# Order of the AV matmuls over two column tiles in a sliding-window attention and SwiGLU kernel

## The chip, the cores and the metric

The kernel runs on one core of a Trainium2 chip. The metric is the device time of one execution in microseconds (us). Times are medians over several executions. A profile is one execution taken by the hardware profiler; its span is about 1.7 us shorter than the timed figure of the same run. All runs quoted here were classed as fast (undisturbed) runs.

In the profile, PE is the TensorE's matmul stream and PEld its stream of weight loads; DVE is VectorE, ACT is ScalarE, POOL is GpSimd, and SPq is the queue from which SyncE issues DMAs. "L354" is line 354 of the kernel. The ends of matmuls are modelled, so everything below is argued from their starts.

## The reference

```python
def _attn_ref(q, k, v):                      # (8, 8, 576, 64), float32
    scores = (q @ k.transpose(0, 1, 3, 2)) / sqrt(64)
    mask = |pos_i - pos_j| <= 32             # a window of 65 positions
    attn = softmax(where(mask, scores, -1e9))
    return attn @ v

x = attention output, heads side by side     # (4608, 512)
out = (silu(x @ w_gate) * (x @ w_val)) @ w_out    # d_ff = 1536
```

## The kernel before

Queries are cut into blocks of 64, and each block needs 128 keys. Two query blocks make a *pair* `m`, with 36 pairs in all. The scores are computed transposed (keys on the partitions), passed through exp and multiplied with a 0/1 mask. The result `p` is then the stationary operand of the AV matmul: 128 keys x 64 queries. The moving operand is `v16`, 64 columns of V and two columns of ones, which give the softmax's denominator: 66 columns. The output of the pair's first query block (`i = 0`) goes to PSUM partitions 0-63, and that of the second (`i = 1`) to 64-127. The profile lists both kinds as 128*64 (128 rows x 64 columns of the array). The two kinds are called the two *column tiles* below.

```python
def pair_av(m, pool=None):
    p = pts.pop(m)
    o = (pool or ps_c).tile([128, 2, 512], FP32, ...)      # two halves of 512
    for i in range(2):
        b, t = divmod(2 * m + i, NT)
        for h in range(H):                                 # H = 8
            nc.tensor.matmul(
                out=o[64 * i:64 * i + 64, h // 4, 66 * (h % 4):66 * (h % 4) + 66],
                lhsT=p[:, place(b, h)[0], i, place(b, h)[1], :],
                rhs=v16[b % 2][:, t, h, :],
                start=True, stop=True)
    # VectorE: reciprocal of the denominators, then normalised x16[m]
    ...

def pair_xt(m, on_pe=False):     # x16[m] is turned into xT, by a DMA transpose or (early) on PE
    ...
```

The two halves of `o`, 512 floats a partition each and chosen by `h // 4`, are called banks below.

The scores (`s_ps`, L306) alternate between two *row* tiles (listed as 64*128: 64 rows x 128 columns), one matmul to each in turn. The rest of PE's work is the FFN: `gv_ps` (L391) and `ob` (L405), on the full 128 x 128 array with 512 columns. The FFN of a chunk of 512 tokens is interleaved with the attention of the next batch, in eight slots:

```python
for j in range(1, NCH):
    ffn1(j)                                       # 96 matmuls, gv_ps
    ...
    groups = {1: ((), (0, 1)), 3: ((0,), (2, 3)), 5: ((1, 2), (4,)), 7: ((3, 4), ())}
    for slot in range(8):
        at_a, at_s = groups.get(slot, ((), ()))   # AV of these pairs, scores of those
        done = [todo[i] for i in at_a if i < n]
        for i, m in enumerate(done):
            pair_av(m, ps_a if i else None)
        for i in at_s: ...pair_scores(todo[i])
        for m in done:
            pair_xt(m)
        ffn2_sub(j, slot // 2, slot % 2)          # 6 matmuls, ob
```

So AV matmuls come in blocks: 16 where one pair stands alone, 32 where two follow one another.

Of the kernel before, what the change touches and what calls it, by code (L numbers as in the profile page):

```python
# [132 lines left out]
def kernel(  # L133
# [12 lines left out]
    B, H, S, D = q.shape  # L146
# [4 lines left out]
    NT = S // 64  # L151
# [145 lines left out]
    def place(b, h):  # L297

        return (h % 4 // 2, 2 * (h // 4) + h % 2) if b < 2 else (h % 2, h // 2)
# [47 lines left out]
    def pair_av(m, pool=None):  # L347
        p = pts.pop(m)
        o = (pool or ps_c).tile([128, 2, 512], FP32, tag="a" if pool is ps_a else "c",
                                name="o_ps")  # L350
        for i in range(2):
            b, t = divmod(2 * m + i, NT)
            for h in range(H):
                nc.tensor.matmul(  # L354
                    out=o[64 * i:64 * i + 64, h // 4, 66 * (h % 4):66 * (h % 4) + 66],
                    lhsT=p[:, place(b, h)[0], i, place(b, h)[1], :],
                    rhs=v16[b % 2][:, t, h, :],
                    start=True, stop=True)
        ov = o[:, :, 0:264].rearrange("p a (h e) -> p a h e", e=66)
        r = rall[:, m, :].rearrange("p (a h) -> p a h", a=2)  # L360
        nc.vector.reciprocal(out=r, in_=ov[:, :, :, 64])  # L361
        x16s[m] = xpool.tile([128, 2, 4, D], FP16, tag="x", name="x16")
        nc.vector.tensor_tensor(out=x16s[m], in0=ov[:, :, :, 0:D],
                                in1=r.unsqueeze(3).to_broadcast([128, 2, 4, D]),
                                op=ALU.mult)
# [140 lines left out]
    quad_mask((2, 3), 1)  # L506
    idle_mms(4)
    pair_av(0)
    pair_av(1, ps_a)
    idle_mms(4)  # L510
    pair_av(2, ps_a)
    pair_av(3)

# [125 lines left out]
```

## Time and profile before

The median before is 341.45 us (341.18 to 341.92, 4 runs). The page of its profile (engines: busy time, share of the span and instructions; then the chain of work that ended last, as shares of the span by engine and by line):

```profile
span 339.8 us, 6448 instructions
PE 327.0 (96%) x2592; PEld 159.8 (47%) x2592; DVE 157.9 (46%) x288; ACT 155.9 (46%) x223; POOL 106.6 (31%) x139
...
PE 94%; DVE 1%; ACT 1%; DMA 1%; issue 1%; POOL 0%; POOLq 0%
PE gv_ps L391 55%; PE ob L405 27%; PE o_ps L354 4%; PE s_ps L306 3%; PE warm L437 2%; PE qk_ps L281 1%; ACT xT L262 1%; DMA xT<-x_1758 1%; PE ob L424 1%; DVE p_t L344 1%; DVE v_103 L265 0%; PE xt_ps L378 0%; DVE mask L202 0%; ACT osb L413 0%; DVE osb_4022 L265 0%
```

PE is the bound: it is on the chain for 94% of the span. The AV matmuls (`o_ps`, L354) are 4% of it, so no ordering of them can gain more than that.

The one DMA in the list of PE's waits (total us, times, longest), just before an FFN:

```profile
PE gv_ps L391 <- DMA xT<-x_1758: 0.3, 1, 0.3
```

The most telling view is the timeline of PE in one 16-block whose two query blocks fall in different batches, so that the two tiles read differently named V buffers (v_103 for `i = 0`, v_104 for `i = 1`). The columns are start, time from the first start to the last end, engine, line, operation and tiles, shapes and count; consecutive starts of the same kind are merged:

```profile
120.99 0.38 PE L405 MATMUL ob<-wo_128,hT 128*128 128x512 f16 x1
121.30 0.34 PE L354 MATMUL o_ps<-v_103,p_t 128*64 128x66 f16 x5
121.45 0.22 PE L354 MATMUL o_ps<-v_104,p_t 128*64 128x66 f16 x1
121.48 0.20 PE L354 MATMUL o_ps<-v_103,p_t 128*64 128x66 f16 x1
121.51 0.20 PE L354 MATMUL o_ps<-v_104,p_t 128*64 128x66 f16 x1
121.51 0.19 PE L354 MATMUL o_ps<-v_103,p_t 128*64 128x66 f16 x1
121.54 0.19 PE L354 MATMUL o_ps<-v_104,p_t 128*64 128x66 f16 x1
121.54 0.19 PE L354 MATMUL o_ps<-v_103,p_t 128*64 128x66 f16 x1
121.58 0.32 PE L354 MATMUL o_ps<-v_104,p_t 128*64 128x66 f16 x5
121.83 0.26 PE L306 MATMUL s_ps<-qT_102,kT_100 64*128 64x64 f16 x5
```

The program has eight v_103, then eight v_104. The chip started the first v_104 when five v_103 had started and three had not, and from there on it ran both tiles side by side. Matmuls of *different* column tiles overtook one another; within a tile the names do not tell the eight apart, and their order there is taken as the program's. The single starts of this block, in ns from its first:

```
i = 0:    0   52   88  120  152  181  215  248
i = 1:                          158  210  246  279  311  340  375  407
```

Counted from its own first start, each row has the same rhythm within 2 ns: 0, 52, 88, 120 or 121, 152 or 153, 181 or 182, 215 to 217, 248 or 249. A tile takes about 249 ns from the first to the last start of its eight matmuls, whether the other runs beside it or not. The second tile only starts 158 ns late, and 158 + 249 = 407. Around the block, the first AV matmul starts 309 or 310 ns after the `ob` before it, where one full-array matmul mostly starts 215 or 216 ns after another, and the next matmul starts 125 to 127 ns after the last AV start (all blocks of this profile from 50 us on, without the one at 60 us).

### The profile page before, as it was taken

The numbers are of one execution on the slowest core, as the hardware profiler recorded it, in microseconds if no ns is written. First come the engines' busy times: TensorE is split into PE (matmuls) and PEld (weight loads), VectorE is DVE, ScalarE is ACT, GpSimd is POOL, SyncE is SP. The second block draws the span as 40 slices with busy tenths as digits, with TensorE's granted clock in tenths as the row PEclk, the third lists the DMA queues.
The fourth block names the chain that finished last, engine by engine and source line by source line (L and its number), as shares of the span: only waits on it lengthen the run. The fifth ranks groups of instructions, "written<-read, shape, count | busy, mean of one in ns | idle before, by whom it ended". The sixth has DMA issues, their size and how long they took to land.

```text
span 339.8 us, 6448 instructions
## 1 busy us (share of the span) xinstructions
PE 327.0 (96%) x2592; PEld 159.8 (47%) x2592; DVE 157.9 (46%) x288; ACT 155.9 (46%) x223; POOL 106.6 (31%) x139
## 2 busy tenths in 40 slices
PE   6889999999999999999999999999999999999993
PEld 3444545444544454445444454455445544444442
DVE  3744365336624763466345644564446634403310
ACT  2964576535543464337333743373336443223321
POOL 8973875146204710463045503560000000000000
PEclk9999999999999999999999999999999999999997
DMA  7999999799969996999599949998530420020012
GB/s 274 169 212 301 212 158 200 126 131 111 147 148 149 99 136 138 131 129 129 151 125 127 130 122 130 152 108 150 111 62 33 106 65 1 33 93 0 2 63 70
DMA packets 152981, 41.92 MB, mean 123 GB/s; under 512 B 140528, under 2 KB 146416, under 8 KB 152944
## 3 DMA queue, kind: packets, MB, share of 16 engines
q0 software_dynamic: 100640, 16.52, 67.7%
q1 hardware_dynamic: 52304, 24.92, 31.4%
q8 instruction: 22, 0.36, 0.5%
q14 instruction: 15, 0.12, 0.1%
HBM read 37.75 MB, written 9.44 MB: 139 GB/s over the span
## 4 chain that ended last, share of the span: by engine, by line
PE 94%; DVE 1%; ACT 1%; DMA 1%; issue 1%; POOL 0%; POOLq 0%
PE gv_ps L391 55%; PE ob L405 27%; PE o_ps L354 4%; PE s_ps L306 3%; PE warm L437 2%; PE qk_ps L281 1%; ACT xT L262 1%; DMA xT<-x_1758 1%; PE ob L424 1%; DVE p_t L344 1%; DVE v_103 L265 0%; PE xt_ps L378 0%; DVE mask L202 0%; ACT osb L413 0%; DVE osb_4022 L265 0%
## 5 line engine op out<-in xcount | busy, mean ns | idle before, releaser
L398 DVE TENSOR_TENSOR hT<-ssb,gv_ps 128x512 f16<-128x512 f16 x108 | 74.3, 688 | 122.4 <-ACT ssb L397 122.1
L397 ACT ACTIVATE ssb<-gv_ps 128x512 f16<-128x512 f32 x108 | 64.5, 597 | 112.7 <-PE gv_ps L391 110.4
L391 PE MATMUL gv_ps<-xT,wg_126 128*128 128x512 f16 x432 | 110.8, 379 | 1.2 <-ACT xT L262 0.8
L391 PE MATMUL gv_ps<-xT,wv_127 128*128 128x512 f16 x432 | 110.9, 379 | 0.0
L405 PE MATMUL ob<-wo_128,hT 128*128 128x512 f16 x420 | 97.3, 380 | 0.0
L391 PEld LDWEIGHTS <-wv_127 128*128 128x128 f16 x432 | 42.3, 98 | 51.0
L391 PEld LDWEIGHTS <-wg_126 128*128 128x128 f16 x432 | 41.9, 98 | 51.6 <-issue 2.8
L405 PEld LDWEIGHTS <-hT 128*128 128x128 f16 x420 | 38.6, 98 | 43.6
L223 POOL DMA_DIRECT2D tok<-in_q_dram x30 | 25.4, 847 | 83.3 <-DMA qT_101<-tok 45.9
L312 ACT ACTIVATE p_t<-s_ps 128x1024 f16<-128x1024 f32 (+1 forms) x40 | 35.3, 937 | 12.3 <-PE s_ps L306 12.2
L413 ACT ACTIVATE osb<-ob 128x512 f32<-128x512 f32 x35 | 21.0, 600 | 41.7 <-PE ob L405 40.6
L223 POOL DMA_DIRECT2D tok<-in_k_dram x30 | 25.3, 843 | 21.3 <-DMA kT_99<-tok 5.0
L322 DVE TENSOR_TENSOR p_t<-p_t,mask 128x1024 f16<-128x1024 f16 x32 | 22.1, 692 | 13.8 <-ACT p_t L312 13.8
L354 PEld LDWEIGHTS <-p_t 128*64 128x64 f16 x576 | 15.4, 110 | 10.6 <-issue 5.9
L361 DVE RECIPROCAL rall<-o_ps 128x8 f32<-128x8 f32 x36 | 7.3, 204 | 21.1 <-PE o_ps L354 21.0
L437 PE MATMUL warm<-mask 128*128 128x512 f16 x26 | 8.9, 467 | 2.9 <-DVE mask L202 2.9
L242 POOL DMA_DIRECT2D v_103<-in_v_dram x12 | 11.4, 956 | 0.5 <-issue 0.5
L354 PE MATMUL o_ps<-v_103,p_t 128*64 128x66 f16 x288 | 10.1, 197 | 1.1 <-DVE p_t L344 1.1
L242 POOL DMA_DIRECT2D v_104<-in_v_dram x12 | 10.6, 896 | 0.0
L397 ACT ACT_TABLE_LOAD x8 | 10.3, 1283 | 0.1
L265 DVE COPY v_103<-v_103 64x512 f16<-64x512 f16 x26 | 9.9, 381 | 0.8
L265 DVE COPY v_104<-v_104 64x512 f16<-64x512 f16 x28 | 9.4, 335 | 0.9
(137 smaller groups left out, 156.3 us busy)
## 6 DMA issues: line engine op xcount, KB each, us to landing
out_dram<-osb SPq DMA_DIRECT2D x35, 256.0 KB, 2.4
tok<-in_q_dram POOLq DMA_DIRECT2D x24, 128.0 KB, 4.9
tok<-in_k_dram POOLq DMA_DIRECT2D x24, 128.0 KB, 5.0
qk_st<-in_q_dram SPq DMA_DIRECT2D x4, 576.0 KB, 6.9
qk_st<-in_k_dram SPq DMA_DIRECT2D x4, 576.0 KB, 8.7
v_103<-in_v_dram POOLq DMA_DIRECT2D x12, 128.0 KB, 5.4
wo_128<-in_moe_w_out_dram POOLq DMA_DIRECT2D x4, 384.0 KB, 21.3
v_104<-in_v_dram POOLq DMA_DIRECT2D x12, 128.0 KB, 4.2
```

The source lines that it names most:

```text
L223: nc.gpsimd.dma_start(out=t[0:n].rearrange("p (h d) -> p h d", d=D), in_=src[b].rearrange("h s d -> s h d")[128 * m:128 * m + n])
L242: nc.gpsimd.dma_start(out=dst[:, 2 * m, :, 0:D], in_=src[128 * m - 32:128 * m + 96])
L265: nc.vector.tensor_copy(out=o, in_=i)
L312: nc.scalar.activation(out=o, in_=s, func=AF.Exp, bias=0.0, scale=1.0 / float(D) ** 0.5)
L322: nc.vector.tensor_tensor(out=flat, in0=flat, in1=mask, op=ALU.mult)
L354: nc.tensor.matmul(out=o[64 * i:64 * i + 64, h // 4, 66 * (h % 4):66 * (h % 4) + 66], lhsT=p[:, place(b, h)[0], i, place(b, h)[1], :], rhs ...
L391: nc.tensor.matmul(out=gv[:, i, :], lhsT=w[:, g, 128 * fk:128 * fk + 128], rhs=xts[j][:, g, :], start=(g == 0), stop=(g == GS - 1))
L397: nc.scalar.activation(out=ssb, in_=gv[:, 0, :], func=AF.Silu, bias=0.0, scale=1.0)
L398: nc.vector.tensor_tensor(out=hts[j][:, fk, :], in0=ssb, in1=gv[:, 1, :], op=ALU.mult)
L405: nc.tensor.matmul(out=ob, lhsT=hts[j][:, fk, 128 * sub:128 * sub + 128], rhs=wo16[:, fk, :], start=(fk == 0), stop=(fk == FKS - 1))
L413: nc.scalar.activation(out=osb, in_=ob, func=AF.Copy, bias=0.0, scale=1.0)
L437: nc.tensor.matmul(out=ob, lhsT=mf[:, 0:128], rhs=mf[:, 0:512], start=True, stop=True)
```

## The change

The intent is to keep both column tiles busy all the time by giving each its next matmul in turn, instead of eight heads of one tile and then eight of the other.

```diff
-        for i in range(2):
-            b, t = divmod(2 * m + i, NT)
-            for h in range(H):
+        for h in range(H):
+            for i in range(2):
+                b, t = divmod(2 * m + i, NT)
                 nc.tensor.matmul(
                     out=o[64 * i:64 * i + 64, h // 4, 66 * (h % 4):66 * (h % 4) + 66],
```

No instruction is added or removed; only PE's order within L354 changes. Below, this order is called *strict turns*.

## The prediction

> **What bounds the kernel.** TensorE. The page gives PE 327.0 us of 339.8 (96%), and the chain that ended last is 94% PE; PE's waits sum to under 8 us, of which 0.3 after 120 us. The AV matmuls (o_ps, L354) are 4.4% of that chain. What shortens PE's AV stretches shortens the program nearly one for one, except where something else starts the next PE stretch.
>
> **AV now.** The 576 AV matmuls stand in 13 blocks of 32 (two pairs) and 10 of 16. By single starts in the timeline, a lone column tile steps every 32 ns: weight load, matmul 26 ns later, next weight load 2 ns later. But where the program changes tile, the second tile starts while the first still has three matmuls to run. The block at 121.30 us, whose two tiles read different v buffers, shows it: five v_103, then v_104 and v_103 in turns, two matmuls per 31 ns step, then five v_104 alone. So a 16-block is 5+3+5 = 13 steps (407 ns, first to last start), a 32-block 5+3+2+3+2+3+5 = 23 steps (726 ns). Part of the overlap is there already.
>
> **The change.** The order comparison shows the same instructions, with PE's order within L354 alone changed. In strict turns every step should carry two matmuls: 8 and 16 steps. The score matmuls (L306), which alternate row tiles, show the shape: starts 3 ns apart, then 26. With each block's start-up (steps of 52 and 36 ns, then 32), a 16-block takes 251 ns to its last start (saves 156), a 32-block 507 (saves 219). The 309 ns before the first AV start and 126 after the last stay. [...]
>
> **On the critical path.**
> - 11 blocks of 32 and 9 of 16 from 50 to 270 us, PE-bound: 11 x 0.219 + 9 x 0.156 = 3.8 us.
> - Blocks at 14.8 and 17.9 us: nothing. VectorE works without pause from the last masks (to 16.8) to x_413 (20.3), which gates the FFN at 21.48.
> - Block at 60.5 us: nothing. The FFN after it waits for ScalarE's xT.
> - At 131.6 us PE waited 0.33 us for the DMA of x_1758. PE comes earlier there, the DMA only in part: 0.3 us given back.
>
> 3.8 - 0.3 = 3.5 us: 341.3 - 3.5 = **337.8 us** (1.0% less), 80% range 336.6 to 339.3. Chances: faster by over 2% 0.01, within 2% 0.98, slower 0.01. Over 2% needs 6.8 us, more than alternation can remove.
>
> **What would show it.** L354 starts in couples 2 to 5 ns apart, every 30 to 32 ns; block time (first AV start to next PE instruction) from 852 to about 633 ns, and 535 to about 380. FFN and score stretches unchanged; first FFN still at about 21.5 us. The wait for xT's DMA from 0.33 to about 0.6 us.
>
> **What would make it wrong.** The couples now write one PSUM bank at once, where today's overlapping ones write different banks. [...] If they took turns, the gain would be zero or negative, as the present overlap would go too. Likewise if the look-ahead fails in strict turns. A small shift can also put other DMA transposes on the path (at 95.9 us xT's landing leads its use by about 0.2 us).

That the two tiles of a couple may write one bank at once was the assumption until experiment 3. The step of a lone tile is stated from single starts: over the block at 121.30 us its matmul starts 26 to 33 ns after its weight load (2 ns for the first), and the next load 1 to 3 ns after that.

## The result

The changed kernel takes 338.06 us (337.96 to 338.52, 4 runs) against 341.45 us. The ratio is 0.9902, 95% interval 0.9885 to 0.9919. Ratios here are the mean time of one kernel's fast runs over that of the other's of the same rounds, so they are not quite the ratios of the medians quoted. The prediction said 337.8 us.

The page after:

```profile
span 336.4 us, 6448 instructions
PE 322.8 (96%) x2592; PEld 155.0 (46%) x2592; DVE 158.1 (47%) x288; ACT 156.0 (46%) x223; POOL 106.2 (32%) x139
...
PE 90%; DMA 4%; DVE 2%; ACT 1%; issue 1%; SPq 1%
PE gv_ps L391 56%; PE ob L405 26%; PE o_ps L354 3%; PE s_ps L306 3%; DMA qk_st<-in_k_dram 2%; DMA xT<-x 2%; ACT xT L262 1%; PE qk_ps L281 1%; DVE p_t L344 1%; PE ob L424 1%; DVE x L363 0%; SPq L215 0%; PE warm L437 0%; PE xt_ps L378 0%; DVE t L265 0%
```

L354's share went from 4% to 3%. DMA's went from 1% to 4%: 2% is the input at the program's start, which landed later in this profile (the last half of K at 10.27 us, 9.70 before), and 2% is xT, of which more below. The same 16-block as above:

```profile
120.33 0.38 PE L405 MATMUL ob<-wo,hT 128*128 128x512 f16 x1
120.64 0.45 PE L354 MATMUL o_ps<-v,p_t 128*64 128x66 f16 x16
121.02 0.26 PE L306 MATMUL s_ps<-qT,kT 64*128 64x64 f16 x6
```

From the first AV start to the score matmul after it are now 0.38 us, not 0.53. (This profile leaves the buffer numbers out, so the 16 are one line.) The single starts, in ns, read as couples in program order:

```
i = 0:    0   53   88  121  153  183  217  249
i = 1:    3   56   92  123  156  185  219  252
```

Each tile's rhythm is what it was. The lag went from 158 to 3 ns, and 3 + 249 = 252.

A 32-block (two pairs), before and then after:

```profile
128.98 0.92 PE L354 MATMUL o_ps<-v_104,p_t 128*64 128x66 f16 x32
129.83 0.60 PE L405 MATMUL ob<-wo_128,hT 128*128 128x512 f16 x2
```

```profile
127.96 0.70 PE L354 MATMUL o_ps<-v,p_t 128*64 128x66 f16 x32
128.59 0.39 PE L405 MATMUL ob<-wo,hT 128*128 128x512 f16 x1
```

From the first AV start to the FFN's next matmul it was 0.85 us and is now 0.64.

### Where the 3.5 us of the span came from

I matched PE's stretches of the two traces one by one and noted by how much the new trace leads the old at the start of each.

| Stretch | Lead gained, ns |
|---|---|
| from the program's start to the first FFN (21.48 us before, 21.51 after) | -32 |
| 11 blocks of 32 from 50 us on: 851-853 ns to 636-642 ns | +2345 |
| 9 blocks of 16 from 86 us on: 533-535 ns to 378-381 ns | +1400 |
| from the transposes on PE through the AV block to the second FFN (58 to 61 us) | -23 |
| the third FFN (95.9 us before): new wait for the DMA of xT | -247 |
| the fourth FFN (131.6 us before): its wait for the DMA of xT, a little shorter | +47 |
| all other PE stretches together | +10 |
| **sum** | **+3500** |

The same entry after the change:

```profile
PE gv_ps L391 <- DMA xT<-x: 0.4, 2, 0.3
```

The list now has two waits for the DMA of xT, where it had one. The new one, at 95 us, first before and then after:

```profile
94.53 1.47 PE L405 MATMUL ob<-wo_128,hT 128*128 128x512 f16 x6
95.92 0.38 PE L391 MATMUL gv_ps<-xT,wg_126 128*128 128x512 f16 x1
```

```profile
93.63 1.47 PE L405 MATMUL ob<-wo,hT 128*128 128x512 f16 x6
95.27 1.02 PE L391 MATMUL gv_ps<-xT,wg 128*128 128x512 f16 x4 [0.17 <-DMA xT<-x]
```

The six `ob` matmuls take the same time. From their first start to the FFN it was 1.39 us and is now 1.64. The chain of waits after the change, cut to these microseconds (start, duration, what), says why:

```profile
89.99 0.42 PE o_ps L354 x16
...
90.43 0.22 DVE rall L361
...
90.68 0.69 DVE x L363
91.37 0.12 DVE rall L361
...
91.52 0.70 DVE x L363
92.22 0.39 SPq L374
...
92.69 2.44 DMA xT<-x
...
95.27 0.81 PE gv_ps L391 x3
```

Two pairs leave PE together, VectorE normalises them one after the other (0.9 us each), and SyncE issues their two transposes one after the other. The second transpose stands behind the first at SPq for 0.39 us and then takes 2.44 us to land. The chain hangs on the first pair of its AV block: from the start of that block the landing came after 5.33 us before and comes after 5.21 now, 0.12 less. PE's own way to the same point got 0.36 us shorter, by the whole of that block (0.21) and the AV block after it (0.16). The difference, 0.24, is the new wait.

### The profile page after: what moved, and what is told of

The parts are those of the page before. It is cut to its first block, busy times and chain, and to the rows that moved or that the text cites. A ratio compares the mean times of both kernels' runs of the same rounds, so it can differ in the third digit from the quotient of the medians.

```text
span 336.4 us, 6448 instructions
## 1 busy us (share of the span) xinstructions
PE 322.8 (96%) x2592; PEld 155.0 (46%) x2592; DVE 158.1 (47%) x288; ACT 156.0 (46%) x223; POOL 106.2 (32%) x139
## 4 chain that ended last, share of the span: by engine, by line
PE 90%; DMA 4%; DVE 2%; ACT 1%; issue 1%; SPq 1%
PE gv_ps L391 56%; PE ob L405 26%; PE o_ps L354 3%; PE s_ps L306 3%; DMA qk_st<-in_k_dram 2%; DMA xT<-x 2%; ACT xT L262 1%; PE qk_ps L281 1%; DVE p_t L344 1%; PE ob L424 1%; DVE x L363 0%; SPq L215 0%; PE warm L437 0%; PE xt_ps L378 0%; DVE t L265 0%
## 5 line engine op out<-in xcount | busy, mean ns | idle before, releaser
L391 PE MATMUL gv_ps<-xT,wg 128*128 128x512 f16 x432 | 110.8, 379 | 1.4 <-ACT xT L262 1.0
L391 PE MATMUL gv_ps<-xT,wv 128*128 128x512 f16 x432 | 110.9, 379 | 0.0
L405 PE MATMUL ob<-wo,hT 128*128 128x512 f16 x420 | 97.3, 380 | 0.0
L391 PEld LDWEIGHTS <-wg 128*128 128x128 f16 x432 | 41.9, 98 | 51.9 <-issue 3.2
L391 PEld LDWEIGHTS <-wv 128*128 128x128 f16 x432 | 42.2, 98 | 51.0
L363 DVE TENSOR_TENSOR x<-o_ps,rall 128x512 f16<-128x512 f32 x36 | 24.9, 692 | 1.2
L242 POOL DMA_DIRECT2D v<-in_v_dram x24 | 21.5, 901 | 0.5 <-ACT p_t L312 0.3
L265 DVE COPY v<-v 64x512 f16<-64x512 f16 x54 | 19.3, 358 | 1.7
L354 PEld LDWEIGHTS <-p_t 128*64 128x64 f16 x576 | 11.2, 110 | 10.4 <-issue 5.5
L354 PE MATMUL o_ps<-v,p_t 128*64 128x66 f16 x576 | 14.0, 196 | 0.7 <-DVE p_t L344 0.7
L306 PE MATMUL s_ps<-qT,kT 64*128 64x64 f16 x576 | 12.2, 191 | 0.4 <-DVE kT L265 0.4
```

Of the source, the lines that this page charges most:

```text
L242: nc.gpsimd.dma_start(out=dst[:, 2 * m, :, 0:D], in_=src[128 * m - 32:128 * m + 96])
L306: nc.tensor.matmul(out=s[:, e, c, :], lhsT=kT[b % 2][half, g, 64 * t:64 * t + 128], rhs=qT[b % 2][half, g, 64 * t:64 * t + 64], start=True ...
L354: nc.tensor.matmul(out=o[64 * i:64 * i + 64, h // 4, 66 * (h % 4):66 * (h % 4) + 66], lhsT=p[:, place(b, h)[0], i, place(b, h)[1], :], rhs ...
L363: nc.vector.tensor_tensor(out=x16s[m], in0=ov[:, :, :, 0:D], in1=r.unsqueeze(3).to_broadcast([128, 2, 4, D]), op=ALU.mult)
L391: nc.tensor.matmul(out=gv[:, i, :], lhsT=w[:, g, 128 * fk:128 * fk + 128], rhs=xts[j][:, g, :], start=(g == 0), stop=(g == GS - 1))
L405: nc.tensor.matmul(out=ob, lhsT=hts[j][:, fk, 128 * sub:128 * sub + 128], rhs=wo16[:, fk, :], start=(fk == 0), stop=(fk == FKS - 1))
```

## The experiments

The theory (A), the reading of the starts above: each column tile runs at its own pace, and PE looks ahead over about four matmuls that have not started and starts the first one whose tile is free. The order in the program then sets only the lag of the second tile. In a run of eight the second tile's first matmul comes into view when the fifth of the run starts (152 ns in the block above), hence the 158 ns.

Rivals: only neighbours in the program overlap, so that strict turns are needed (C); the gain is in the weight loads alone, and the matmuls of the two tiles still take turns; or the new order also pays or saves something in PSUM, because the two matmuls of a couple now write the same bank.

Block times below are from the first AV start to the next PE instruction, over the blocks from 50 us on without the one at 60 us. The kernel before has 533-535 and 851-853 ns, strict turns 378-381 and 635-642 ns.

### 1. Strict turns again, for a yardstick

> The changed kernel itself, unaltered, run again on the chip of the other runs of this call, as their yardstick. Expected 0.990 of the kernel before (338.0 us), blocks of 16 and 32 AV matmuls 379 and 636 to 642 ns from first start to the next PE instruction. The wait of PE for the DMA of xT near 95 us (0.25 us in the first profile) should be there again if it follows from PE coming earlier, and be gone if it was chance.

It measured 338.30 us (337.57 to 340.14), ratio 0.9905 (0.9876 to 0.9935). Blocks took 378-379 and 635-642 ns. Near 95 us the gap before the FFN was 528 ns (546 in the first profile, 298 before the change). Near 131 us this run waited much longer than either of the first two profiles:

```profile
PE gv_ps L391 <- DMA xT<-x: 1.0, 1, 1.0
```

The wait at 95 us came back and the one at 131 us varies. The spread of the runs is wide, 2.6 us; more on that below. So for differences under 1 us I rely on block times and gaps in the traces.

### 2. Runs of four

```diff
-        for h in range(H):
-            for i in range(2):
+        for i, h in [(i, h0 + h) for h0 in (0, 4) for i in range(2) for h in range(4)]:
```

> Four heads of one column tile, then four of the other. Theory A (PE looks ahead over four matmuls that have not started, and starts the first whose column tile is free; the gain is the filled steps): all steps stay filled, 16- and 32-blocks within 15 ns of strict turns (379, 640 ns), time within 0.1% of strict turns. Rival B (look-ahead of three): one lone step per block, about +30 to +50 ns a block, +0.6 to +1.0 us in all (338.6 to 339). Rival C (only neighbours in the program overlap, so strict turns are needed): most of the gain is lost, 16-blocks near 500 ns, 340.5 us or more.

It measured 338.52 us, ratio 0.9914 (0.9890 to 0.9937). Blocks took 406-409 and 663-665 ns. The 16-block of above (in this kernel the line is L353):

```profile
120.72 0.48 PE L353 MATMUL o_ps<-v,p_t 128*64 128x66 f16 x16
121.13 0.55 PE L306 MATMUL s_ps<-qT,kT 64*128 64x64 f16 x26
```

Rival C is out: most of the gain is kept although only three of the fifteen neighbours in a pair's 16 matmuls are of different tiles. But 28 ns a block is more than the 15 I had allowed A, and is close to what I had written down for B, a look-ahead of three (30 to 50 ns). The single starts decide it (assigned to tiles by program order and each tile's rhythm, since the names are the same):

```
i = 0:    0   53   89  122  155  184  219  251
i = 1:   14   66  102  134  166  214  249  282
```

The second tile starts 14 ns after the first, with three of the first tile's matmuls still to start; a look-ahead of three would have shown it only with the first tile's second start, at 53 ns. So four fits and three does not. The second tile loses its step at the border of its two runs. Until the first tile's fifth matmul starts at 155, the second tile's fifth is the fifth in line of those not started, out of view; its weight load is issued at 159, where within a run it comes right after the start before (134). I read this as the tile having run empty, for its next step is as long as a start-up step: 166 to 214, 48 ns, nearly as at the start of the blocks shown (0 to 52 or 53); the first tile's step at that place is 29. So a run of four sits just at the edge of the view, and costs 11 ns at the start and about 18 at the border, once.

The starts do not show what in the chip makes this view of four. Other rules of issue could give the same ones, and no run here tells them apart; "look-ahead of four" below stands for the pattern of the starts alone.

### 3. The two matmuls of a couple in different banks

```diff
-        for h in range(H):
-            for i in range(2):
+        for i, h in [(i, (h + 4 * i) % H) for h in range(H) for i in range(2)]:
```

> Strict turns, but the second tile takes its heads in the order 4 5 6 7 0 1 2 3, so that the two matmuls of a couple never write the same PSUM bank. If sharing a bank costs something, couples get closer than the 31 ns of strict turns and blocks shrink below 379 and 640 ns. If it costs nothing (expected): blocks within 10 ns, time within 0.1% of strict turns.

It measured 338.27 us, ratio 0.9900 (0.9875 to 0.9925). Blocks took 380-382 and 637-641 ns:

```profile
122.48 0.45 PE L353 MATMUL o_ps<-v,p_t 128*64 128x66 f16 x16
122.87 0.32 PE L306 MATMUL s_ps<-qT,kT 64*128 64x64 f16 x10
```

Writing the same bank at once costs nothing that shows: the blocks do not shrink when the banks differ (380-382 and 637-641 ns here, 378-381 and 635-642 with one bank). The prediction's main worry is answered.

### 4. Strict turns only in the three blocks called off the critical path

```diff
-        for h in range(H):
-            for i in range(2):
+        turns = m in (0, 1, 2, 3, 8)
+        for i, h in ([(i, h) for h in range(H) for i in range(2)] if turns
+                     else [(i, h) for i in range(2) for h in range(H)]):
```

> Strict turns only in pairs 0, 1, 2, 3 and 8, the three blocks that the prediction called off the critical path (14.8, 17.9 and 60.5 us); all others as before. Expected if that reading is right: their AV stretches get shorter, but the FFN after them starts where it did, and the time is that of the kernel before within 0.1 us (341.3 to 341.5). If every saved PE nanosecond counted: 0.25 + 0.22 + 0.16 = 0.6 us faster (340.8).

It measured 341.36 us against 341.43, ratio 1.0009 (0.9976 to 1.0042; one of its six runs took 344.25). That agrees with the reading, but the interval is too wide to exclude 0.6 us. The trace says more. The block at 60 us, in the kernel before and then here (L355 and L392 are the same lines, shifted):

```profile
60.52 0.60 PE L354 MATMUL o_ps<-v_104,p_t 128*64 128x66 f16 x16
61.28 0.38 PE L391 MATMUL gv_ps<-xT,wg_126 128*128 128x512 f16 x1 [0.15 <-ACT xT L262]
```

```profile
60.01 0.45 PE L355 MATMUL o_ps<-v,p_t 128*64 128x66 f16 x16
60.76 0.81 PE L392 MATMUL gv_ps<-xT,wg 128*128 128x512 f16 x3 [0.31 <-ACT xT L262]
```

The AV stretch is 0.15 us shorter, the wait for ScalarE's xT is 0.16 us longer, and the FFN starts 0.75 us after the block's start in place of 0.76. A gain off the critical path turned into a wait, whole.

The two blocks at the start are nearly, not wholly, off the path. From the end of the last mask on VectorE to the first FFN it was 4.68 us before; it is 4.50 us here, and 4.50 or 4.51 in the three profiles of strict turns, the two of experiment 7's version and those of runs of two and four. (It is 4.86 in the profile of the other bank, whose start was disturbed, as told under the spread of the runs, and 4.73 with 132 columns.) VectorE, in the kernel before:

```profile
17.60 0.20 DVE L361 RECIPROCAL rall<-o_ps 128x8 f32<-128x8 f32 x1
...
18.57 0.21 DVE L361 RECIPROCAL rall<-o_ps 128x8 f32<-128x8 f32 x1
```

From one reciprocal to the next are 0.97 us here, where the other pairs take 0.85 and this step takes 0.84 after the change: VectorE did wait briefly for pair 2's AV, which is most of the difference. About 0.17 us were to be had at the start, where I had said none. In the first pair of profiles this is covered by inputs that came later: the last mask was done at 16.80 us before and at 17.01 after.

### 5. Runs of sixteen

`pair_av` takes both pairs of a block, and runs all of tile 0 before tile 1 (cut to the core):

```diff
-        for h in range(H):
-            for i in range(2):
+        for i in range(2):
+            for (m, _), p, o, h in [(*x, h) for x in zip(pairs, pp, oo) for h in range(H)]:
```

> Longer runs than before: where two pairs stand together, sixteen matmuls of the first column tile, then sixteen of the second; single pairs stay in runs of eight, as before. Theory A (look-ahead of four): the second tile starts with the thirteenth start of the first, so a 32-block takes 408 ns + 6 + 504 ns + 126 = about 1044 ns instead of the 852 of before; 16-blocks 535. 11 blocks on the path x 0.192 = 2.1 us slower than before, about 343.4 us (ratio 1.006), less up to 0.3 where PE waited for a DMA. If the order of the tiles did not matter: 341.4.

It measured 344.41 us against 341.84, ratio 1.0073 (1.0058 to 1.0089): slower than the kernel before. Blocks took 534-535 and 1046-1050 ns; the estimate for 32-blocks was 1044, that for the ratio 1.006.

```profile
130.51 1.12 PE L354 MATMUL o_ps<-v,p_t 128*64 128x66 f16 x32
131.56 0.39 PE L409 MATMUL ob<-wo,hT 128*128 128x512 f16 x1
```

In this block the thirteenth start is at 411 ns and the fourteenth, of the second tile, at 417; a look-ahead of three would have put that a step (32 ns) later. The 11 blocks on the path lose 2.17 us together. The rest, about 0.5 us, was lost at the start, where the last mask to the first FFN took 5.15 us (4.68 before): VectorE waited longer for pairs 0 and 2.

### 6. Twice the columns

```diff
-                    out=o[64 * i:64 * i + 64, h // 4, 66 * (h % 4):66 * (h % 4) + 66],
+                    out=o[64 * i:64 * i + 64, h // 4, 66 * (h % 4):66 * min(h % 4 + 2, 4)],
                     lhsT=p[:, place(b, h)[0], i, place(b, h)[1], :],
-                    rhs=v16[b % 2][:, t, h, :],
+                    rhs=v16[b % 2][:, t, h:h // 4 * 4 + min(h % 4 + 2, 4), :],
```

> Strict turns, but each AV matmul of heads 0-2 and 4-6 streams 132 columns instead of 66 (the next head's columns come along and are overwritten by the next matmul, so the result is right); weight loads unchanged. From the FFN's 216 ns for 512 columns a column takes 0.42 ns, 66 more 28 ns. If the two tiles stream at the same time: +28 ns for each of 6 of 8 couples, 16-blocks about 545 ns, 32-blocks about 970, in all 9 x 0.165 + 11 x 0.33 = +5.1 us on strict turns (343.1). If the streams share one path and only weight loads are hidden: a wide couple takes at least 111 ns, +80 each, about +14 us (352). If the weight load sets the step, less than +5.

The result is correct, at 342.58 us, ratio 1.0022 (1.0007 to 1.0038). Blocks took 530 and 938-939 ns, against 545 and 970 expected:

```profile
121.83 0.60 PE L354 MATMUL o_ps<-v,p_t 128*64 128x132 f16 x16
122.36 0.32 PE L306 MATMUL s_ps<-qT,kT 64*128 64x64 f16 x10
```

Over strict turns that is +151 ns for the six wide couples of a 16-block, 25 ns each (28 if streaming alone set the step). After the first, a wide couple steps in 57 to 60 ns. Two streams of 132 columns one after the other, at the FFN's 0.42 ns a column (216 ns for 512 columns), would need 111 ns by estimate. So the two tiles stream at the same time, and hiding weight loads is not the whole gain. As a couple of 66 columns steps in 31 ns where the same estimate gives 28 for its streaming, there is little left in it but fewer columns.

### 7. Other slots: a version that takes the new wait away

The chain at 95 us puts two transposes behind one another. This version moves the AV of pair 1 one slot earlier and, to keep the PSUM buffers free, the scores of pair 3 one slot later:

```diff
-        groups = {1: ((), (0, 1)), 3: ((0,), (2, 3)), 5: ((1, 2), (4,)), 7: ((3, 4), ())}
+        groups = {1: ((), (0, 1)), 3: ((0, 1), (2,)), 5: ((2,), (3, 4)), 7: ((3, 4), ())}
```

> Strict turns, and the slots of a stage filled otherwise: AV of pairs 0 and 1 with the scores of 2, then AV of 2 with the scores of 3 and 4 (was: AV 0 with scores 2 3, then AV 1 2 with scores 4). Same matmuls and as many blocks, but pair 1 is turned by the DMA a slot earlier, so the two xT transposes no longer stand behind one another before the FFN of the next chunk. Expected if the waits of PE near 95 and 130 us (0.25 and 0.3 us) come from that queue: both vanish, 0.4 to 0.6 us faster than strict turns (337.5), unless the scores of pair 4 now come too late for its AV. If the waits have another cause: 338.0.

It measured 337.80 us, ratio 0.9887 (0.9868 to 0.9905). No wait of PE for a DMA of xT is left in the list of waits. At 95 us:

```profile
93.66 1.47 PE L405 MATMUL ob<-wo,hT 128*128 128x512 f16 x6
94.97 1.03 PE L391 MATMUL gv_ps<-xT,wg 128*128 128x512 f16 x4
```

The FFN follows 1.31 us after the first `ob`, less even than the 1.39 of before, and the 131 us wait is gone as well. So with the pair in front of it moved a slot earlier, the transpose that gates the FFN comes in time, here (issued at 92.08 us, landed at 94.50, 0.48 us before the FFN's start) and in the second series below (experiment 8). Strict turns did not run in this series; against the kernel before, the ratio is 0.9887, where the series of experiment 1 gave strict turns 0.9905.

### 8. Runs of two, and the slots beside strict turns

Runs of two are experiment 2 with `h0 in range(0, H, 2)` and two heads. They are meant to check the explanation of the 28 ns.

> Two heads of one column tile, then two of the other. Runs of four cost 25 to 28 ns a block over strict turns: in the trace the second tile falls one step behind at the border of two runs, where its next matmul comes into view of the look-ahead of four only when the first tile starts. If that is the cause, a run of two never reaches the end of the view: 16-blocks 379 to 390 ns, 32-blocks 636 to 650, time within 0.1% of strict turns. If instead each change between unequal neighbours costs, it stays near the 407 and 664 ns of runs of four.

Blocks took 383-387 and 641-645 ns: about 5 ns over strict turns, against 28 for runs of four. A run well inside the look-ahead costs next to nothing. The time, 338.97 us (ratio 0.9916, 0.9899 to 0.9933; strict turns in the same series 0.9915), is no good measure here: the profiled run took 341.12 us and lost clock (below), and waited 1.0 us for xT.

> The changed kernel unaltered, as the yardstick of the next run on the same chip. Expected 0.990 of the kernel before; PE waits about 0.25 us for the DMA of xT near 95 us again, and near 131 us between 0 and 1 us, by chance.

It measured 338.39 us, ratio 0.9915 (0.9902 to 0.9928). The gap before the FFN was 536 ns near 95 us and 958 ns near 131 us.

> The other filling of the slots once more, beside strict turns on the same chip. In its first run no wait of PE for xT's DMA was left and the ratio to the kernel before was 0.9887. Expected 0.3 to 0.8 us faster than strict turns (0.25 us near 95 us for certain, the rest by what the transpose near 131 us does in the yardstick).

It measured 337.94 us, ratio 0.9892 (0.9877 to 0.9907), again without a wait for xT's DMA. Beside strict turns in this one series the slots came out 0.45 us of median ahead, where 0.3 to 0.8 were expected. The intervals of the ratios overlap, so the time alone does not prove it. What the profiles show is that the waits are gone: 1.06 us in the one profile of strict turns (gaps of 536 and 958 ns where 216 is undisturbed), of which the second varies from run to run. It is the fastest version tried, by the medians.

### All runs side by side

| AV order | 16-block, ns | 32-block, ns | median, us | ratio |
|---|---|---|---|---|
| runs of 16 | 535 (run of 8) | 1048 | 344.41 | 1.0073 |
| runs of 8 (before) | 535 | 852 | 341.45 | 1 |
| runs of 8, strict turns in three early blocks | 534 | 852 | 341.36 | 1.0009 |
| runs of 4 | 407 | 664 | 338.52 | 0.9914 |
| runs of 2 | 385 | 644 | 338.97 | 0.9916 |
| strict turns (three series) | 379 | 638 | 338.06, 338.30, 338.39 | 0.9902, 0.9905, 0.9915 |
| strict turns, different banks | 381 | 639 | 338.27 | 0.9900 |
| strict turns, 132 columns | 530 | 938 | 342.58 | 1.0022 |
| strict turns, other slots (two series) | 379 | 638 | 337.80, 337.94 | 0.9887, 0.9892 |

### The spread of the runs

Runs of one kernel differed by up to 3.8 us within one series (340.49 to 344.25, experiment 4). Three of the profiles fell on slower executions (339.38, 340.17 and 341.12 us), and each has one stretch of 3.41 us with a granted clock of 0.50: from 21.6 us in the second run of the other slots, from 9.2 in the other bank, from 22.2 in runs of two. The stretch 20:24 us (bounds; length; busy time of PE, PEld, DVE, ACT and POOL with instruction counts; granted clock; DMA share; GB/s), first in the second run of the other slots, then in the third series of strict turns:

```profile
20.00:24.00 4.00, 3.12 (x14) 1.25 (x14) 0.47 (x5) 2.81 (x4) 2.81 (x5) 0.71 1.31 203
```

```profile
20.00:24.00 4.00, 3.11 (x19) 1.48 (x18) 0.34 (x6) 3.20 (x5) 2.42 (x5) 1.00 1.31 205
```

The mean clock of these 4 us was 0.71 in the one (0.50 from 21.6 us on) and 1.00 in the other, while the waits of PE before it were alike, none over a microsecond between 12 and 24 us. What decides it was not tested. In the other bank's profile the clock is not the whole story: its inputs came late as well (the last half of K landed at 11.58 us, 9.70 in the kernel before), PE waited 2.2 us for one of them, and the first FFN started 1.9 us later. All this happens early, away from the AV blocks compared here.

## Why the prediction was right

**The bound.** PE-bound, with AV 4% of the chain: right. From the first FFN on, the new trace gains almost only in L354.

**The mechanism.** "Part of the overlap is there already" was the step that mattered. Counting AV as wholly serial before would have promised 16 steps of 32 ns per 32-block, half a microsecond; the starts showed 23 steps, not 32, and so 7 to be saved. The prediction's 156 and 219 ns a block stand against 154-157 and 209-216 measured. Runs of 16, 8, 4, 2 and 1 order themselves as a look-ahead of four says: 1048, 852, 664, 644 and 638 ns. What I called 13 and 23 steps is better said as the lag plus a tile's own 249 or 504 ns; the sums are the same.

**The critical path.** The sum over 20 blocks was 3.8 us; measured, 3.75. The block at 60 us gave nothing, as predicted. For the two blocks at the start I had also said nothing; about 0.17 us were there (experiment 4), masked in the first profile by inputs that landed later. In that pair of profiles the two cancelled.

**The 0.3 us given back.** The size was right by luck, for the place was wrong. I had put it at 131.6 us, where PE already waited 0.33 us. That wait turned out to vary without any help from the change: the gap before that FFN was 706 ns in the profile before, 658, 1397 and 958 in three profiles of strict turns, and too short to show a wait in experiment 4, which has the order of before in all blocks near it. What the change gave back by rule was 0.25 us at 95 us, in all three profiles of strict turns, in those of the other bank and of runs of four (gaps of 525 to 546 ns, against 298 and 300 in the two profiles with runs of eight there), and more in that of runs of two (806). There I had named only a risk, and had read the distance from xT's landing to its use as a lead of about 0.2 us. It was no lead. In the kernel before the transpose landed at 95.785 us and the FFN started at 95.921, 0.136 us later; the same 0.136 us lie between landing and start in the waits that are listed (131.493 and 131.629 before, 95.131 and 95.267 after). And the FFN's first matmul came 298 ns after the last `ob`, where it comes after 215 or 216 when nothing holds it (experiment 7). So PE already waited 0.08 us there before the change, too short to be listed, and whatever PE gained on the transpose after that was lost whole. With the pair in front moved a slot earlier (experiment 7) both waits are gone; how long the second one lasts in a given run was not traced to a cause.

**What would make it wrong.** None of it came about: one bank for both tiles costs nothing that shows (experiment 3: 379 ns a 16-block with one bank, 381 with two), and the couples in strict turns start 2 to 4 ns apart in the block shown.

## What to carry to other kernels

Where small matmuls go to different column tiles of the array, issue them in turns: here each tile kept its own pace (about 249 ns from the first to the last of its eight starts), runs of two cost about 5 ns a block, runs of four 28, and runs of eight left the second tile idle for 158 ns at the start of the block shown. Before costing such a change, read the single starts in the trace, for the ends of the runs may already overlap, as they did here; the gain is the lag that is left, not half the time. And when the bounding engine gets shorter by tenths of a microsecond, look at what arrives just in time for its next stretch. Compare the gap there with that of the same place in an undisturbed stretch (298 against 216 ns): a wait too short for the list showed that the DMA had no lead left. Here a quarter of a microsecond went back to it, and was won back by moving the pair in front of it one slot earlier.
